# A spectral filter and a maxout layer on one core: the start-up of batch 0 and batch 1 replanned, filter split at two thirds, x in 8-token pieces

## The chip, the cores and the metric

The kernel runs on one NeuronCore of a Trainium2 chip. The metric is the device time of one execution in microseconds; the verdicts compare medians of runs of the two kernels on the same chip. The engines are named as in the profile: PE (TensorE matmuls), PEld (TensorE weight loads), DVE (VectorE), ACT (ScalarE), POOL (GpSimd) and SP (SyncE, which here only issues DMAs).

## What is computed

```python
def reference(x, filt_r, filt_i, moe_w1, moe_w2, moe_w_out):   # x: 8 x 3072 x 256 fp32
    X = np.fft.rfft(x, axis=1)                                 # 1537 frequencies, 256 channels
    Y = X * (filt_r + 1j * filt_i)[None]
    y = np.fft.irfft(Y, n=3072, axis=1).reshape(8 * 3072, 256)
    h1, h2 = y @ w1, y @ w2                                    # 256 -> 1024
    return np.maximum(h1, h2) @ w_out                          # 1024 -> 256
```

The kernel uses max(h1, h2) = h2 + relu(h1 - h2): Wd = w1 - w2, and M = w2 @ w_out goes straight from y to the output.

## The kernel before

**The transform.** 3072 = 96 x 32. A forward transform has two stages: f1 or s1 multiplies over the 96 rows (tables C1, CT), the result `at` goes to DRAM (`ad`) and is read back transposed as `bt`; s2 multiplies with the table U over the 32 columns and gives `px`. `product` multiplies px with the filter F (real and imaginary part) and gives `pq`. The inverse has s3 (tables VP and VQ), a copy `zt`, a way through DRAM (`zd`, read back as `zr` by z_read) and s4, which gives `y_`. A batch has six groups v of s2, product and s3; a *visit* n of a batch does s3 of group n-1, s2 and products of group n, and s1 for some chunks c ("quads") of the batch after it.

**Batch 0** does not go through DRAM: s1t, t1 (PE transposes into bt[0]), s2, products, s3t into zT and t2 (transposes into zr[0]), all written out in order at L538 to L614. Its x comes in eight POOL DMAs (`load_x`, L77, fp32 to bf16 on the way), the filter in eighteen (`load_f`, L95), in two halves h of six groups w each, one for the first and one for the second three v. The filter rows stand twice in F: `copy_f` doubles the first half on DVE, `dma_f` the second half by four SP DMAs. `fix_f` mends three rows on POOL. `stage_x` copies a px out of PSUM by ACT so that POOL can do a product; the groups in POOLED (L572) have their second product on POOL, the others on DVE. `spin(n)` is n matmuls whose result nobody reads, and s3t begins with one or two such matmuls (L497).

**Weights.** load_w reads w1 and w2 as fp32 (SP DMAs); w2 lies in two of the three buffers XF that later take x. prep_wd makes Wd on POOL in two halves, cast_w2 makes bf16 w2, prep_t and prep_m make M.

**The loop** (L665) has 64 blocks tt of 384 tokens, eight steps j each. A step does moe_h (two matmuls `ph` and a relu into gt, on DVE where `on_v` says so, else on ACT), then what `mid` plans for this step (the visits), then some matmuls `po` of moe_o of the block before, then what `todo` plans (f1, t2, reads, loads, folds). Steps are counted 0 to 63 within a batch of eight blocks. plan_f1 and plan_f2 put the work of the next batch on steps: f1 of batch 1 (16 chunks of two tokens, each reading half of an `xb` tile), f1_read (the bt read), the visits, z_read, s1_read, and for the batch after that load_xf (SP DMAs into XF) and fold (two POOL operations, sum and difference, into `xsd`).

**Order.** The schedule is by hand: every engine runs its instructions in the order of the code, and each DMA queue (SP's and POOL's) issues in that order too. A POOL or SP instruction that waits holds back all that stands behind it. SP issues F doubling, weights, ad writes, XF loads, bt and zr reads and zd writes; POOL issues x and filter loads, w_out and the output writes, and computes products, Wd, memsets and folds. POOL DMAs carry eight completion semaphores in turn, so the ninth waits for the first to land, and so on.

The lines that place batch 1's work in batch 0 are:

```python
    plan_f1(0, 1, (0, 1, 1, 2, 3, 3, 4, 5, 6, 7, 8, 8, 9, 9, 10, 10), 11)
    plan_f2(0, (22, 26, 30, 34, 38, 42, 46, 54), ((0, 1), (2,), (3,), (), (), (4,), (5,), (6, 7)),
            (8, 9, 10, 19, 21, 24, 27, 30), (13, 16, 19, 24, 27, 30, 33, 36))
```

Of the kernel before, what the change touches and what calls it, by code (L numbers as in the profile page):

```python
# [8 lines left out]
FP32 = mybir.dt.float32  # L9
BF16 = mybir.dt.bfloat16  # L10
# [16 lines left out]
def kernel(  # L27
# [34 lines left out]
    dram = ctx.enter_context(tc.tile_pool(name="dram", bufs=2, space=bass.MemoryType.DRAM))  # L62
    CT = const.tile([128, 2, 64], BF16)
    XF = [const.tile([128, 2, 2, D], FP32, name="XF%d" % k) for k in range(3)]
    xpool = ctx.enter_context(tc.tile_pool(name="xpool", bufs=8))
    bpool = ctx.enter_context(tc.tile_pool(name="bpool", bufs=2))
    pqpool = ctx.enter_context(tc.tile_pool(name="pqpool", bufs=6))
    ps = ctx.enter_context(tc.tile_pool(name="ps", bufs=6, space=bass.MemoryType.PSUM))
# [5 lines left out]

    xb = {}

    def load_x(b, c):  # L77
        t_ = xpool.tile([NP, 4, D], BF16, tag="xb", name="xb")
        src = x[b].rearrange("(p m) d -> p m d", m=NM)
        G.dma_start(out=t_, in_=src[:, 4 * c:4 * c + 4, :])  # L80
        xb[b, c] = t_

    def load_xf(b, c):
        src = x[b].rearrange("(h p m) d -> p h m d", h=2, m=NM)
        for g in range(2):
            nc.sync.dma_start(out=XF[(8 * b + c) % 3][64 * g:64 * g + 48], in_=src[:, :, 4 * c + 2 * g:4 * c + 2 * g + 2, :])

    def fold(b, c):
        t_ = xpool.tile([128, 2, 2, D], BF16, tag="xb", name="xsd")
        f = XF[(8 * b + c) % 3]  # L90
        G.tensor_tensor(t_[:, 0], f[:, 0], f[:, 1], OP.add)  # L91
        G.tensor_tensor(t_[:, 1], f[:, 0], f[:, 1], OP.subtract)  # L92
        xb[b, c] = t_

    def load_f(h):  # L95
        w0 = 6 * h
        for g in range(2):
            for ri, f in enumerate((filt_r, filt_i)):
                k0 = 24 * g + 2 * w0
                src = bass.AP(f.tensor, f.offset + k0 * D, [[96 * D, 16], [D, 12], [1, D]])  # L100
                G.dma_start(out=F[64 * g:64 * g + 16, ri, w0:w0 + 6].rearrange("p w s d -> p (w s) d"), in_=src)
                n0 = 1 if k0 == 0 else 0
                src = bass.AP(f.tensor, f.offset + (96 - k0 - n0) * D, [[96 * D, 16], [-D, 12 - n0], [1, D]])
                G.dma_start(out=F[64 * g + 16:64 * g + 32, ri, w0:w0 + 6].rearrange("p w s d -> p (w s) d")[:, n0:12],  # L104
                            in_=src)
                if n0:
                    src = bass.AP(f.tensor, f.offset + 48 * D, [[96 * D, 16], [1, D]])
                    G.dma_start(out=F[16:32, ri, 0, 0], in_=src)

    def copy_f(h, g, ri, engine):  # L110
        w0 = 6 * h
        o_, i_ = F[64 * g + 32:64 * g + 64, ri, w0:w0 + 6], F[64 * g:64 * g + 32, ri, w0:w0 + 6]
        if engine is S:
            S.activation(o_, i_, AF.Copy)
        else:
            engine.tensor_copy(o_, i_)

    def dma_f(h, g, ri):
        w0 = 6 * h
        nc.sync.dma_start(out=F[64 * g + 32:64 * g + 64, ri, w0:w0 + 6], in_=F[64 * g:64 * g + 32, ri, w0:w0 + 6])  # L120

    FN = init.tile([33, D], FP32)

# [19 lines left out]
    load_x(0, 0)  # L143
# [3 lines left out]
    load_x(0, 1)  # L147
# [3 lines left out]
    load_x(0, 2)  # L151
    G.iota(cid, pattern=[[1, 128]], base=0, channel_multiplier=0, allow_small_or_imprecise_dtypes=True)
    for c in range(3, 8):
        load_x(0, c)
    load_f(0)
    load_f(1)
    load_fn()
# [99 lines left out]
            S.activation((VQ if q else VP)[:, 6 * h:6 * h + 6, s], pv[s], AF.Copy)  # L257


    w1f = init.tile([128, 2, HID], FP32)  # L260
    w2f = [XF[h].rearrange("p c m d -> p c (m d)") for h in range(2)]

    def load_w(h):
        js = slice(512 * h, 512 * h + 512)
        nc.sync.dma_start(out=w1f[:, :, js], in_=moe_w1.rearrange("(c p) j -> p c j", p=128)[:, :, js])
        nc.sync.dma_start(out=w2f[h], in_=moe_w2.rearrange("(c p) j -> p c j", p=128)[:, :, js])

    def cast_w2(h, c):
        V.tensor_copy(w2b[:, c, 512 * h:512 * h + 512], w2f[h][:, c])

    def load_wo():
        G.dma_start(out=Wo, in_=moe_w_out.rearrange("(c p) j -> p c j", p=128))

    def prep_wd(h, engine):
        js = slice(512 * h, 512 * h + 512)
        engine.tensor_tensor(Wd[:, :, js], w1f[:, :, js], w2f[h], OP.subtract)

    def prep_t(jp):
        pt = ps.tile([128, 4, D], BF16, tag="ps", name="pt")
# [134 lines left out]
    gt = {}  # L414
    on_v = {(i, j) for i in range(8) for j in range(8)
            if (j in (1, 4, 6) if 2 < 8 * i + j < 11 else j in (1, 2, 4, 6, 7) if 8 * i + j < 22
                else j == 3 if 8 * i + j < 48 else j in (1, 3, 6))}

    def moe_h(tt, j):
        if j == 0:  # L420
# [73 lines left out]
    def s3t(v, pq):  # L494
        pool, tag = (ps, "ps") if v >= 4 else (pso, "po")
        pz = [pool.tile([128, 2, 2, 2, 2, NM], FP32, tag=tag, name="pt%d" % g) for g in range(2)]
        for _ in range(2 if v == 1 else 1):  # L497
            TE.matmul(pz[0].rearrange("p i s r c m -> p (i s r c m)"), W1[:, 0:128], W1, start=True, stop=True)
        for i in range(2):
            for s in range(2):  # L500
                for dc in range(2):
                    for q, tab in enumerate((VP, VQ)):
                        for g in range(2):
                            TE.matmul(pz[g][:, i, s, :, dc], pq[s][64 * g:64 * g + 64, q, i, 128 * dc:128 * dc + 128],  # L504
                                      tab[64 * g:64 * g + 64, 2 * v + i, s].rearrange("p (r m) -> p r m", r=2),
                                      start=(q == 0), stop=(q == 1))
# [34 lines left out]
    tables_u()  # L541
    for g in range(2):
        for ri in range(2):
            dma_f(1, g, ri)
    for h in range(2):
        load_w(h)
    spin(12)
# [9 lines left out]
    for n in range(6):  # L557
        t1(n, S if n % 2 else V)
    put_v(0, 0, table_v(0, 0))
    copy_f(0, 0, 0, V)  # L560
    copy_f(0, 0, 1, V)
    fix_f()
    copy_f(0, 1, 0, V)
    copy_f(0, 1, 1, V)
    xs = {}

    def stage_x(v):
# [1 line left out]
        S.activation(t_, pxs[v][1], AF.Copy)  # L569
        xs[v] = t_  # L570

    POOLED = (0, 2, 3)  # L572

    def products(v):
        pq = [product(V, v, 0, pxs[v][0])]
        pq.append(product(G, v, 1, xs[v]) if v in POOLED else product(V, v, 1, pxs[v][1]))
        return pq
# [16 lines left out]
    pxs[4] = s2(0, 4)  # L594
    pqs[3] = products(3)
    s3t(0, pqs[0])
    pxs[5] = s2(0, 5)
    load_x(1, 0)
    load_x(1, 1)
    pqs[4] = products(4)  # L600
    s3t(2, pqs[2])
    pqs[5] = products(5)
    for v in (3, 4, 5):
        s3t(v, pqs[v])
    spin(3)
# [11 lines left out]
    zpool = ctx.enter_context(tc.tile_pool(name="zpool", bufs=3))  # L617
    ypool = ctx.enter_context(tc.tile_pool(name="ypool", bufs=3))
    gpool = ctx.enter_context(tc.tile_pool(name="gpool", bufs=2))
    opool = ctx.enter_context(tc.tile_pool(name="opool", bufs=2))  # L620
    s4(0)
    spin(2)

# [88 lines left out]
```

## Time and profile before

| | us |
|---|---|
| median of 3 runs | 508.45 (506.44 to 508.6) |
| the profiled execution | 509.96 |
| its span in the profile | 508.2 |
| DVE, ACT, POOL busy | 331.0, 308.7, 259.6 |

The page also has the chain that ended last and the costliest groups:

```profile
PE 89%; DMA 4%; POOL 3%; DVE 1%; ACT 1%; issue 1%; SPq 0%; POOLq 0%; DVEq 0%
...
L452 PE MATMUL po<-Wo,gt 128*128 128x256 bf16 x1536 | 261.2, 273 | 0.0
L429 ACT ACTIVATE gt<-ph 128x384 bf16<-128x384 f32 x324 | 158.4, 495 | 144.4 <-PE ph L425 143.8
...
L365 DVE TENSOR_TENSOR pq<-px,F 128x1024 bf16<-128x1024 f32 x93 | 109.3, 1219 | 31.6 <-PE px L359 27.2
```

The first line shares out the chain by engine. A group's row has line, engine, operation, output and inputs, shape and count, then its busy time, the mean of one in ns, and the idle time of its engine just before it with what ended most of it.

### The profile page before, as it was taken

What the parts mean: (1) busy time and instruction counts of PE and PEld (TensorE: products, weight loads), DVE (VectorE), ACT (ScalarE), POOL (GpSimd) and SP (SyncE); (2) the same over time, 40 slices, a digit from 0 to 9 for tenths busy, and PEclk for the clock granted to TensorE, in tenths of its full rate; (3) what the DMA queues carried; (4) which work ended last, traced back from release to release, by engine and by line L of the source; (5) the groups of instructions that cost most, each with busy time, mean ns of one, the idle gap of its engine ahead of it and who ended that gap; (6) DMA issues with size and microseconds to landing.
All of it is one profiled execution on the core that took longest, in us unless ns stands there. A gap on an engine that the chain in (4) does not pass through costs nothing.

```text
span 508.2 us, 13046 instructions
## 1 busy us (share of the span) xinstructions
PE 492.7 (97%) x5302; PEld 364.0 (72%) x5305; DVE 331.0 (65%) x515; ACT 308.7 (61%) x628; POOL 259.6 (51%) x341
## 2 busy tenths in 40 slices
PE   7689989999999999999999999999999999999997
PEld 3456757777777777777777777777777777777775
DVE  7866668546875677557774677657774687555443
ACT  5756467766784576646774576646774465544442
POOL 6886378565645386539645466537742221222220
PEclk9858999999999999999999999999999999999999
DMA  7979697988799878895789778897769426511112
GB/s 123 172 219 177 206 300 220 253 253 193 219 251 238 185 245 219 243 261 167 214 229 239 191 233 183 260 232 201 218 177 227 117 105 166 165 65 63 63 63 83
DMA packets 75439, 97.06 MB, mean 191 GB/s; under 512 B 7314, under 2 KB 53651, under 8 KB 74707
## 3 DMA queue, kind: packets, MB, share of 16 engines
q1 hardware_dynamic: 61666, 66.60, 51.7%
q0 software_dynamic: 13712, 29.64, 20.4%
q8 instruction: 41, 0.67, 0.6%
q14 instruction: 20, 0.16, 0.1%
HBM read 53.48 MB, written 47.19 MB: 198 GB/s over the span
## 4 chain that ended last, share of the span: by engine, by line
PE 89%; DMA 4%; POOL 3%; DVE 1%; ACT 1%; issue 1%; SPq 0%; POOLq 0%; DVEq 0%
PE po L452 33%; PE ph L425 32%; PE po L450 8%; PE pz L376 5%; PE py L405 4%; PE pa L333 2%; PE px L359 2%; DMA xb<-in_x_dram 2%; DMA bt<-ad 1%; DVE pq L365 1%; DMA ad<-at 1%; POOL F L104 1%; PE pr L525 1%; POOL xb L80 1%; PE pt L504 1%
## 5 line engine op out<-in xcount | busy, mean ns | idle before, releaser
L452 PE MATMUL po<-Wo,gt 128*128 128x256 bf16 x1536 | 261.2, 273 | 0.0
L429 ACT ACTIVATE gt<-ph 128x384 bf16<-128x384 f32 x324 | 158.4, 495 | 144.4 <-PE ph L425 143.8
L438 POOL DMA_DIRECT2D out_dram<-ot x186 | 102.4, 555 | 183.3 <-DVE ot L464 176.6
L452 PEld LDWEIGHTS <-gt 128*128 128x128 bf16 x1536 | 146.5, 98 | 66.3 <-issue 10.7
L427 DVE TENSOR_SCALAR gt<-ph 128x384 bf16<-128x384 f32 x188 | 103.3, 553 | 64.2 <-PE ph L425 62.3
L365 DVE TENSOR_TENSOR pq<-px,F 128x1024 bf16<-128x1024 f32 x93 | 109.3, 1219 | 31.6 <-PE px L359 27.2
L425 PEld LDWEIGHTS <-Wd 128*128 128x128 bf16 x1024 | 96.7, 98 | 12.7 <-issue 1.1
L91 POOL TENSOR_TENSOR xsd<-XF 128x512 bf16<-128x512 f32 x48 | 61.2, 1276 | 43.5 <-DMA XF<-in_x_dram 13.4
L464 DVE COPY ot<-po 128x512 f32<-128x512 f32 x95 | 65.1, 685 | 24.3 <-PE po L452 19.2
L92 POOL TENSOR_TENSOR xsd<-XF 128x512 bf16<-128x512 f32 x48 | 61.0, 1271 | 0.0
L337 ACT ACTIVATE at<-pa 128x512 bf16<-128x512 f32 x96 | 51.7, 609 | 4.4 <-PE pa L333 4.1
L380 ACT ACTIVATE zt<-pz 128x512 bf16<-128x512 f32 x84 | 45.6, 595 | 11.4 <-PE pz L376 8.4
L405 PE MATMUL py<-G,zr 96*128 96x96 bf16 x512 | 32.7, 207 | 0.0
L405 PEld LDWEIGHTS <-zr 96*128 96x128 bf16 x512 | 29.2, 98 | 2.3 <-DVE zr L528 0.6
L359 PE MATMUL px<-bt,U 64*64 64x256 bf16 x384 | 20.4, 280 | 3.6 <-DMA bt<-ad 2.5
L376 PE MATMUL pz<-pq,VP 64*64 64x256 bf16 x336 | 21.9, 281 | 0.0
L376 PE MATMUL pz<-pq,VQ 64*64 64x256 bf16 x336 | 20.9, 269 | 0.0
L333 PE MATMUL pa<-xsd,CT 64*64 64x512 bf16 x192 | 19.3, 384 | 0.0
L376 PEld LDWEIGHTS <-VP 64*64 64x64 bf16 x336 | 9.7, 105 | 13.3 <-issue 13.3
L359 PEld LDWEIGHTS <-U 64*64 64x64 bf16 x384 | 10.4, 109 | 6.7 <-issue 3.7
L535 PE MATMUL pd<-W 128*128 128x512 bf16 x32 | 11.9, 488 | 1.8 <-DVE zero L137 1.5
L333 PEld LDWEIGHTS <-CT 64*64 64x64 bf16 x192 | 8.3, 105 | 2.4 <-ACT gt L429 1.2
(428 smaller groups left out, 609.7 us busy)
## 6 DMA issues: line engine op xcount, KB each, us to landing
out_dram<-ot POOLq DMA_DIRECT2D x186, 128.0 KB, 3.6
XF<-in_x_dram SPq DMA_DIRECT2D x96, 192.0 KB, 4.9
ad<-at SPq DMA_DIRECT2D x56, 192.0 KB, 3.8
bt<-ad SPq DMA_DIRECT2D x14, 768.0 KB, 11.5
zd<-zt SPq DMA_DIRECT2D x42, 256.0 KB, 2.9
zr<-zd SPq DMA_DIRECT2D x14, 768.0 KB, 7.8
xb<-in_x_dram POOLq DMA_DIRECT2D x16, 192.0 KB, 6.0
w1f<-in_moe_w_dram SPq DMA_DIRECT2D x2, 512.0 KB, 6.1
```

Source lines behind the costliest of these rows:

```text
L91: G.tensor_tensor(t_[:, 0], f[:, 0], f[:, 1], OP.add)
L92: G.tensor_tensor(t_[:, 1], f[:, 0], f[:, 1], OP.subtract)
L337: S.activation(at[:, m0:m0 + 2], pa[g], AF.Copy)
L365: E.tensor_tensor(pq, px.rearrange("p (o i) d -> p o i d", o=1).to_broadcast([128, 2, 2, D]), F[:, :, 2 * v:2 * v + 2, s], OP.mult)
L376: TE.matmul(pz[g][64 * s:64 * s + 64, i], tab[64 * g:64 * g + 64, 2 * v + i, s], pq[s][64 * g:64 * g + 64, q, i], start=(q == 0), stop=(q ...
L405: TE.matmul(py[:, m], zr[b][:, 4 * i + m, 128 * dc:128 * dc + 128], G1, start=True, stop=True)
L425: TE.matmul(ph, Wd[:, dc, 128 * j:128 * j + 128], y_[:, dc], start=(dc == 0), stop=(dc == 1))
L427: V.tensor_scalar(gt[tt][:, j], ph, 0.0, None, OP.max)
L429: S.activation(gt[tt][:, j], ph, AF.Relu)
L438: E.dma_start(out=dst, in_=ot[tt // 2][:, 3 * (tt % 2) + c])
L452: TE.matmul(p_, g_[:, n - 2, blk], Wo[:, n - 2], start=False, stop=(n == 9))
L464: V.tensor_copy(ot[tt // 2][:, e - 1:e + 1], po[0])
```

## The change

- `x_tile`: an xb tile holds eight tokens (two chunks) instead of four, in four buffers instead of eight. `load_x(b, c, n)` loads n chunks in one DMA; batch 0 comes as 1, 1, 2, 2, 2 chunks, batch 1 as four pairs. fold writes halves of such a tile.
- `WP`: the filter's first part has eight groups w (v = 0 to 3), the second four. `double_f` replaces copy_f and dma_f: the first part is doubled on DVE, the second by SP.
- The fp32 weights lie in `WS`, a tile of the zr pool, whose other buffer is zr[0]; XF is free of them.
- POOLED gets v = 4. s3t begins with two idle matmuls for v below 4; after s3t there is one spin fewer (two instead of three).
- In POOL's queue, all four pairs' and w_out's loads and the two prep_wd change order; table_ct (memsets of XF) goes from step 5 to step 2; opool is allocated earlier.
- Batch 0's plan: f1 on steps 0 to 8 instead of 0 to 10, the bt read at step 9 instead of 11, seven visits instead of eight, other steps for XF loads and folds; batch 1's loads and folds every 7 steps instead of 8.
- `on_v`: for blocks' steps 22 to 47 of batch 0, relus j = 1 and 5 on DVE instead of j = 3.

```diff
-    xpool = ctx.enter_context(tc.tile_pool(name="xpool", bufs=8))
+    xpool = ctx.enter_context(tc.tile_pool(name="xpool", bufs=4))
...
+    def x_tile(b, c):
+        if c % 2 == 0:
+            xb[b] = xpool.tile([128, 8, D], BF16, tag="xb", name="xb")
+        return xb[b][:, 4 * (c % 2):4 * (c % 2) + 4]
+
+    def load_x(b, c, n):
+        for k in range(c, c + n):
+            xb[b, k] = x_tile(b, k)[0:NP]
         src = x[b].rearrange("(p m) d -> p m d", m=NM)
-        G.dma_start(out=t_, in_=src[:, 4 * c:4 * c + 4, :])
-        xb[b, c] = t_
+        m0 = 4 * (c % 2)
+        G.dma_start(out=xb[b][0:NP, m0:m0 + 4 * n], in_=src[:, 4 * c:4 * c + 4 * n, :])
...
+    WP = ((0, 8), (8, 12))
+
     def load_f(h):
-        w0 = 6 * h
+        w0, w1 = WP[h]
+        n = 2 * (w1 - w0)
...
-    def copy_f(h, g, ri, engine):
...
-    def dma_f(h, g, ri):
...
+    def double_f(h, g, ri, engine):
+        w0, w1 = WP[h]
+        o_, i_ = F[64 * g + 32:64 * g + 64, ri, w0:w1], F[64 * g:64 * g + 32, ri, w0:w1]
+        if engine is V:
+            V.tensor_copy(o_, i_)
+        else:
+            nc.sync.dma_start(out=o_, in_=i_)
...
-    w1f = init.tile([128, 2, HID], FP32)
-    w2f = [XF[h].rearrange("p c m d -> p c (m d)") for h in range(2)]
+    WS = zrpool.tile([128, 4, HID], FP32, tag="zr", name="WS")
+    w1f, w2f = WS[:, 0:2], WS[:, 2:4]
...
-                else j == 3 if 8 * i + j < 48 else j in (1, 3, 6))}
+                else j in (1, 5) if 8 * i + j < 48 else j in (1, 3, 6))}
...
-        for _ in range(2 if v == 1 else 1):
+        for _ in range(2 if v < 4 else 1):
...
-    copy_f(0, 0, 0, V)
-    copy_f(0, 0, 1, V)
-    fix_f()
-    copy_f(0, 1, 0, V)
-    copy_f(0, 1, 1, V)
+    for g in range(2):
+        for ri in range(2):
+            double_f(0, g, ri, V)
+        if g == 0:
+            fix_f()
...
-    POOLED = (0, 2, 3)
+    POOLED = (0, 2, 3, 4)
...
+    stage_x(4)
     pxs[5] = s2(0, 5)
-    load_x(1, 0)
-    load_x(1, 1)
     pqs[4] = products(4)
+    for c in (0, 2):
+        load_x(1, c, 2)
     s3t(2, pqs[2])
     pqs[5] = products(5)
+    prep_wd(0, G)
     for v in (3, 4, 5):
         s3t(v, pqs[v])
-    spin(3)
-    prep_wd(0, G)
-    load_x(1, 2)
-    load_x(1, 3)
+    spin(2)
+    load_wo()
+    for c in (4, 6):
+        load_x(1, c, 2)
     prep_wd(1, G)
-    load_wo()
-    for c in range(4, 8):
-        load_x(1, c)
...
-    plan(0, 5, table_ct)
+    plan(0, 2, table_ct)
...
-    plan_f1(0, 1, (0, 1, 1, 2, 3, 3, 4, 5, 6, 7, 8, 8, 9, 9, 10, 10), 11)
-    plan_f2(0, (22, 26, 30, 34, 38, 42, 46, 54), ((0, 1), (2,), (3,), (), (), (4,), (5,), (6, 7)),
-            (8, 9, 10, 19, 21, 24, 27, 30), (13, 16, 19, 24, 27, 30, 33, 36))
+    plan_f1(0, 1, (0, 1, 1, 2, 2, 3, 3, 4, 4, 5, 6, 6, 7, 7, 8, 8), 9)
+    plan_f2(0, (22, 26, 30, 34, 38, 42, 46), ((0, 1), (2,), (3,), (4,), (5,), (6,), (7,)),
+            (6, 7, 11, 17, 19, 23, 26, 30), (13, 15, 18, 24, 27, 30, 33, 36))
     for b in range(1, B - 1):
         plan_f2(b, (7, 14, 18, 24, 31, 38, 42) if b > 1 else (14, 18, 24, 30, 34, 39, 42), ((0, 1), (2,), (3,), (4,), (5,), (6,), (7,)),
-                range(-32, 32, 8), range(-22, 42, 8))
+                range(-32, 32, 8) if b > 1 else range(-25, 31, 7), range(-22, 42, 8) if b > 1 else range(-15, 41, 7))
```

More of the change, by code (lines that the diff above doesn't have):

```diff
@@ L75 @@
     xb = {}
-    def load_x(b, c):
-        t_ = xpool.tile([NP, 4, D], BF16, tag="xb", name="xb")
+    def x_tile(b, c):
[5 more added lines that the diff above has]
+            xb[b, k] = x_tile(b, k)[0:NP]
         src = x[b].rearrange("(p m) d -> p m d", m=NM)
-        G.dma_start(out=t_, in_=src[:, 4 * c:4 * c + 4, :])
-        xb[b, c] = t_
+        m0 = 4 * (c % 2)
+        G.dma_start(out=xb[b][0:NP, m0:m0 + 4 * n], in_=src[:, 4 * c:4 * c + 4 * n, :])
     def load_xf(b, c):
@@ L85, in load_xf @@
         for g in range(2):
-            nc.sync.dma_start(out=XF[(8 * b + c) % 3][64 * g:64 * g + 48], in_=src[:, :, 4 * c + 2 * g:4 * c + 2 * g + 2, :])
+            nc.sync.dma_start(out=XF[(8 * b + c) % 3][64 * g:64 * g + 48],
+                              in_=src[:, :, 4 * c + 2 * g:4 * c + 2 * g + 2, :])
     def fold(b, c):
-        t_ = xpool.tile([128, 2, 2, D], BF16, tag="xb", name="xsd")
+        t_ = x_tile(b, c).rearrange("p (s m) d -> p s m d", s=2)
         f = XF[(8 * b + c) % 3]
@@ L99, in load_f @@
                 k0 = 24 * g + 2 * w0
-                src = bass.AP(f.tensor, f.offset + k0 * D, [[96 * D, 16], [D, 12], [1, D]])
-                G.dma_start(out=F[64 * g:64 * g + 16, ri, w0:w0 + 6].rearrange("p w s d -> p (w s) d"), in_=src)
+                src = bass.AP(f.tensor, f.offset + k0 * D, [[96 * D, 16], [D, n], [1, D]])
+                G.dma_start(out=F[64 * g:64 * g + 16, ri, w0:w1].rearrange("p w s d -> p (w s) d"), in_=src)
                 n0 = 1 if k0 == 0 else 0
-                src = bass.AP(f.tensor, f.offset + (96 - k0 - n0) * D, [[96 * D, 16], [-D, 12 - n0], [1, D]])
-                G.dma_start(out=F[64 * g + 16:64 * g + 32, ri, w0:w0 + 6].rearrange("p w s d -> p (w s) d")[:, n0:12],
+                src = bass.AP(f.tensor, f.offset + (96 - k0 - n0) * D, [[96 * D, 16], [-D, n - n0], [1, D]])
+                G.dma_start(out=F[64 * g + 16:64 * g + 32, ri, w0:w1].rearrange("p w s d -> p (w s) d")[:, n0:n],
                             in_=src)
@@ L108, in load_f @@
                     G.dma_start(out=F[16:32, ri, 0, 0], in_=src)
-    def copy_f(h, g, ri, engine):
[L111 to L114, printed above, removed]
-        else:
-            engine.tensor_copy(o_, i_)
-    def dma_f(h, g, ri):
-        w0 = 6 * h
-        nc.sync.dma_start(out=F[64 * g + 32:64 * g + 64, ri, w0:w0 + 6], in_=F[64 * g:64 * g + 32, ri, w0:w0 + 6])
+    def double_f(h, g, ri, engine):
[3 more added lines that the diff above has]
+            V.tensor_copy(o_, i_)
+        else:
+            nc.sync.dma_start(out=o_, in_=i_)
     FN = init.tile([33, D], FP32)
@@ L142 @@
     cid = init.tile([128, 128], FP32)
-    load_x(0, 0)
+    load_x(0, 0, 1)
     G.iota(pid, pattern=[[1, 1]], base=0, channel_multiplier=1, allow_small_or_imprecise_dtypes=True)
@@ L146 @@
            allow_small_or_imprecise_dtypes=True)
-    load_x(0, 1)
+    load_x(0, 1, 1)
     G.iota(kap, pattern=[[2, NW], [24, 2]], base=0, channel_multiplier=0,
@@ L150 @@
     G.iota(jb, pattern=[[1, 16]], base=0, channel_multiplier=0, allow_small_or_imprecise_dtypes=True)
-    load_x(0, 2)
+    load_x(0, 2, 2)
     G.iota(cid, pattern=[[1, 128]], base=0, channel_multiplier=0, allow_small_or_imprecise_dtypes=True)
-    for c in range(3, 8):
-        load_x(0, c)
+    for c in (4, 6):
+        load_x(0, c, 2)
     load_f(0)
@@ L265, in load_w @@
         nc.sync.dma_start(out=w1f[:, :, js], in_=moe_w1.rearrange("(c p) j -> p c j", p=128)[:, :, js])
-        nc.sync.dma_start(out=w2f[h], in_=moe_w2.rearrange("(c p) j -> p c j", p=128)[:, :, js])
+        nc.sync.dma_start(out=w2f[:, :, js], in_=moe_w2.rearrange("(c p) j -> p c j", p=128)[:, :, js])
     def cast_w2(h, c):
-        V.tensor_copy(w2b[:, c, 512 * h:512 * h + 512], w2f[h][:, c])
+        V.tensor_copy(w2b[:, c, 512 * h:512 * h + 512], w2f[:, c, 512 * h:512 * h + 512])
     def load_wo():
@@ L275, in prep_wd @@
         js = slice(512 * h, 512 * h + 512)
-        engine.tensor_tensor(Wd[:, :, js], w1f[:, :, js], w2f[h], OP.subtract)
+        engine.tensor_tensor(Wd[:, :, js], w1f[:, :, js], w2f[:, :, js], OP.subtract)
     def prep_t(jp):
@@ L543 @@
         for ri in range(2):
-            dma_f(1, g, ri)
+            double_f(1, g, ri, nc.sync)
     for h in range(2):
@@ L596 @@
     s3t(0, pqs[0])
+    stage_x(4)
     pxs[5] = s2(0, 5)
-    load_x(1, 0)
-    load_x(1, 1)
     pqs[4] = products(4)
+    for c in (0, 2):
+        load_x(1, c, 2)
     s3t(2, pqs[2])
     pqs[5] = products(5)
+    prep_wd(0, G)
     for v in (3, 4, 5):
         s3t(v, pqs[v])
-    spin(3)
-    prep_wd(0, G)
-    load_x(1, 2)
-    load_x(1, 3)
+    spin(2)
+    load_wo()
+    for c in (4, 6):
+        load_x(1, c, 2)
     prep_wd(1, G)
-    load_wo()
-    for c in range(4, 8):
-        load_x(1, c)
     t2(0, (V, S))
@@ L617 @@
     zpool = ctx.enter_context(tc.tile_pool(name="zpool", bufs=3))
+    opool = ctx.enter_context(tc.tile_pool(name="opool", bufs=2))
     ypool = ctx.enter_context(tc.tile_pool(name="ypool", bufs=3))
     gpool = ctx.enter_context(tc.tile_pool(name="gpool", bufs=2))
-    opool = ctx.enter_context(tc.tile_pool(name="opool", bufs=2))
     s4(0)
```

## The prediction

> **What bounds the kernel now.** I read the page first, then busy time by stage, then the timelines of the stages in which PE is not full, and the landings of single DMAs.
>
> ```profile
> span 508.2 us, 13046 instructions
> PE 492.7 (97%) x5302; PEld 364.0 (72%) x5305; DVE 331.0 (65%) x515; ACT 308.7 (61%) x628; POOL 259.6 (51%) x341
> ...
> 22.00:42.35 20.35, 16.46 (x316) 10.23 (x320) 12.90 (x15) 9.82 (x19) 17.70 (x17) 0.50 0.76 192
> 42.35:65.25 22.90, 22.36 (x195) 16.01 (x193) 16.47 (x31) 13.45 (x25) 10.37 (x15) 1.00 0.86 211
> 65.25:67.85 2.60, 0.12 (x2) 0.00 (x2) 0.00 (x0) 0.49 (x1) 2.58 (x5) 1.00 1.03 309
> 67.85:97.00 29.15, 29.15 (x378) 21.62 (x379) 21.84 (x26) 23.88 (x50) 21.37 (x23) 1.00 0.89 248
> 97.00:440.00 343.00, 343.00 (x3627) 256.33 (x3625) 230.59 (x337) 217.04 (x446) 175.55 (x222) 1.00 0.79 210
> ```
>
> The stage rows give us, then busy time of PE, PEld, DVE, ACT and POOL, the granted clock and the DMA share. From 67.85 us on PE is never idle up to its last matmul at 504.5, so no edit can win there; it can only lose. The change's whole effect is the moment from which PE is continuously full. Ahead of it stand two things: 20 us at half clock (0.50) and a hole of 2.6 us.
>
> ```profile
> 31.12 5.75 DVE L365 TENSOR_TENSOR pq<-px,F 128x1024 bf16<-128x1024 f32 x5 [4.24 <-DMA F<-F]
> ...
> 20.55 6.33 SPq L120 DMA_DIRECT2D F<-F  x4
> ...
> 40.91 2.26 POOL L80 DMA_DIRECT2D xb<-in_x_dram  x4
> ...
> 57.26 0.43 SPq L316 DMA_DIRECT2D ad<-at  x1
> ...
> 61.82 1.73 SPq L322 DMA_DIRECT2D bt<-ad  x2
> 63.59 4.92 SPq L86 DMA_DIRECT2D XF<-in_x_dram  x4
> ...
> 67.85 0.41 PE L359 MATMUL px<-bt,U 64*64 64x256 bf16 x8 [2.48 <-DMA bt<-ad]
> 72.88 0.39 PE L333 MATMUL pa<-xsd,CT 64*64 64x512 bf16 x4
> ```
>
> Columns: start, length, engine, line, operation, and in brackets the idle time before it and who ended it. DVE loses 4.24 us to the second filter half; PE's hole is the wait for bt, whose chain is the last ad write, its landing (4.5 us) and the read (6.0 us). The last row is the second visit's s1, the point against which I count.
>
> **The change, part by part.** All times are from the span's start.
>
> *x in 8-token pieces.* Last x landing now 14.11 (issue 6.18, 7.93 to land). In one piece with its neighbour it leaves s1t twice (0.34 apart) and two spins (0.43) to do: 0.8 late. POOL issues three DMAs of 0.53 fewer, which may land it earlier: between 0 and 0.8, I take +0.4.
>
> *Filter split.* DVE's four doublings cover 4096 instead of 3072 elements: 0.93 each becomes 1.24, +1.2 in all. They start at 18.43+0.4 and end at 23.8. The products follow at 1.15: the first pair ends at 26.1 (24.55 now). Five products, not four, precede the first that needs the second part, so DVE asks for it at 29.55. Now it lands at 26.38+4.6=31.0. POOL ends its issues some 1.5 earlier and the pieces are 128 KB, not 192: 28 to 31, I take 29.5, so DVE ends at 33.0 instead of 36.87.
>
> *Spins and PE.* That gain has no taker, because PE, cold, becomes the end. From the first s3t (26.85) follow: table 0.6, s2 0.65, then three s3t with two spins each (2 x 0.53 + 0.97), s2 0.64 and a wait of 0.65 for zT, and two s3t with one spin (1.50 each). That ends at 38.5 (37.7 now). The spin taken out later gives back 0.43. The first moe_h comes at 42.5, against 42.13.
>
> *Fourth Pool product, order of Pool.* ACT stages it only behind the copies of s3t(0) (ends 30.1): 1.08+0.6, so POOL runs it from 31.8 to 33.9 (2.13). Behind it in POOL's queue: two pairs of x, Wd half 0 (2.36, done 37.4, in time), Wo, two pairs, Wd half 1 (done 41.9; needed at step 4). The x landings: 3.3 fixed plus 0.97 per chunk (4.2 and 4.6 of the first two), so pairs at 39.1 and 41.0; Wo keeps the DMA engines 4.4 (from 41.9 to its landing at 46.27), hence 44.9; the third pair about 46.9. f1 chunk 8 is its reader.
>
> *f1 by step 8 instead of 10.* From c8 to c15 PE does 4.76 (48.54 to 53.3 now) plus what moved in between: s4 0.34, two prep_t 0.88, two ph 0.66, four f1 0.88, that is 7.5. If c8 waits for the pair, c15 ends at 54.4, against 55.86: 1.5 earlier. DVE and ACT have some 11 and 10 us of work in these nine steps against PE's 11, so they can take up to 1 of it.
>
> *bt read ahead.* From c15: copy and issue 1.4, write 3.75 to 4.5 (I take 3.75, the row of a write with two XF loads ahead of it, since the third now comes behind), so the read is issued at 59.6 and lands 5.2 to 6.0 later, 65.2. PE's own path from c15 to the first visit is 11.0, 65.4. The hole is gone: -2.45.
>
> *What is late next.* XF piece 2 (step 11) now queues on SP behind the bt read (step 9). The first XF behind bt took from 61.82 to 71.5, 9.7, its twin 0.5 more; less 0.8 for the loads no longer beside it, 9.4: 69.0. POOL's fold (two of 1.26) ends 71.5. s1 of the second visit, 5.03 behind the first, asks at 70.4. A new wait of 1.0, bounds 0 and 1.8 (without the 0.8). I take 0.5, below the middle, as the 9.7 is measured behind a read that began while four loads were still landing. So this s1 comes at 70.9, 16.5 after c15, where it is 72.88 now, 17.0 after c15. Behind it on POOL wait only out writes, whose ot has two buffers.
>
> *At nothing:* weights in the zr buffer and the earlier memset (POOL at 42 to 50, which nobody awaits before fold at 60); ACT to DVE, three more relus of 0.55 on DVE over 26 steps and four s1 earlier on ACT: DVE 21.8 and ACT 23.9 of 29.15 us in that stage leave room; if a burst closes it, 0.2 a visit, 1.4 at most. opool's place only moves addresses.
>
> **Sum.** -2.45+0.5 is -1.95. The profiled execution took 509.96, 1.76 around its span of 508.2; the median of the runs is 508.45, 1.5 below it. The span becomes 506.25 and the runs 506.5, that is -0.4%.
>
> **The rivals.**
>
> *The clock rises early* (0.23). PE's clock fell at about 21.9 and rose at 42.35, 20.4 us later. With the extra spins PE is without a break from 26.1 to 32.6. If it rises near 32.1, the last s3t ends at 35.5 instead of 38.5 and moe_h starts at 38.7. Where the x pairs are in time as well, c15 ends 12.4 later at 51.1 and the second visit's s1 comes at 51.1+16.5=67.6, 5.2 earlier: 503.2. For it: 39.0 to 42.35, full of spins, did raise the clock. Against: 28.8 to 32.1 was 85% busy and did not, and most of the new stretch is 64-row tiles; and a third pair landing at 46.9 takes it back to the forecast.
> The Trainium skill, TensorE: Matmul & The Clock Gate, Part 1: The HAM clock gate, says that one busy window of about 3.4 us frees the full clock and that the window runs free of the kernel; by it the break-free 6.5 us hold such a window. The trace agrees on the length (20.4 is six of them), not yet on what counts as busy.
>
> *The Pool queue runs late* (0.16, slower). The last filter issues, under DVE's doublings, took 1.05, 0.86 and 1.03 where earlier ones took 0.48 to 0.55, and two landed after 6.1 and 6.0 instead of 4. The doublings now last 5.0. If they hold the last four issues until 23.8, those end at 25.9, land at 31.9, and the doubling DMA at 36.6; the fourth product ends at 38.7 and everything behind it on POOL with it: third pair 51.7, c15 59.2, the second visit's s1 75.7, 2.9 later than now: 511.3. It decides from a product end of about 35.8. Against it: the issues were slowed, not stopped.
> The Trainium skill, SBUF — State Buffer, SBUF: two separate sides, says that a two-port VectorE copy locks GpSimd out so that it cannot write descriptors; by it this rival would be the rule. The slowed issues agree in kind, their 0.5 us in size does not.
>
> *It does nothing* (0.11). Clock cold, c15 at 42.5+12.4=54.9, the write 4.5 and the fold wait in full: 54.9+1.4+4.5+9.4+2.5=72.7, nearly the 72.88 of now: 508.3. The hole would only have moved.
>
> **Chances and range.** Forecast 0.50, of which 0.20 lie below 505.9. 0.5% is 2.5 us, about what a measurement of this kernel can tell from no change (the three runs lie within 2.2). Faster 0.20+0.23=0.43; same 0.30+0.11=0.41; slower 0.16. The range reaches from the early clock (503.0) to a Pool case of less than half its price (509.6); the forecast's own is 504.9 to 507.7.
>
> **What would show it.** Right: no 4.24 stall on DVE; the last s3t near 38 if the clock is still 0.50; a PE wait for xb near c8; bt landing within 0.5 of the first visit; a PE or POOL wait for XF near 70. Wrong: the clock at 1.00 by 33 and c8 unhindered (then faster), the last F issue after 23 (then slower), or any PE idle time after 75.

## The result: 6.6 us slower

The changed kernel takes 514.06 us (median of 6 runs, 512.56 to 515.34); the kernel before took 507.49 beside it (6 runs, 506.07 to 509.65). The ratio is 1.0125, 95% interval 1.0093 to 1.0157. The forecast was 506.5, range 503.0 to 509.6: the sign was wrong, and the time lies outside the range.

The profiled execution of the changed kernel took 514.36, its span 512.6. First the page, then the busy time by stage, in the same stages as before:

```profile
span 512.6 us, 13010 instructions
PE 492.4 (96%) x5302; PEld 363.9 (71%) x5307; DVE 337.9 (66%) x517; ACT 307.2 (60%) x626; POOL 262.1 (51%) x335
```

```profile
22.00:42.35 20.35, 14.85 (x332) 8.69 (x337) 15.33 (x15) 12.08 (x25) 19.30 (x16) 0.75 0.72 183
42.35:65.25 22.90, 19.43 (x145) 13.27 (x144) 16.66 (x25) 10.81 (x20) 9.56 (x10) 0.85 0.71 169
65.25:67.85 2.60, 2.60 (x26) 2.02 (x25) 2.19 (x4) 0.42 (x2) 2.60 (x3) 1.00 1.12 331
67.85:97.00 29.15, 28.33 (x360) 20.85 (x359) 23.26 (x30) 22.29 (x48) 22.32 (x24) 1.00 0.89 237
97.00:440.00 343.00, 341.92 (x3626) 255.61 (x3624) 229.91 (x336) 215.69 (x443) 177.83 (x224) 1.00 0.79 211
```

PE's busy time in the whole kernel is the same (492.4 against 492.7), so it is idle time that grew. The hole of 2.6 before bt is gone, as meant: PE is busy in all of 65.25 to 67.85. The first cold stretch is shorter: a clock of 0.75 over 20.35 us means half clock for 10.2 us, where it was all 20.35. But between 42.35 and 65.25 PE did 195 matmuls before and does 145 now, and the clock there is 0.85, so there is a second cold stretch of 6.9 us. After 67.85, where PE had no idle time before, 0.82 and 1.08 us are lost.

The timeline of DVE, and then that of POOL, of the changed kernel in the stage that lost (start, length, engine, line, operation):

```profile
40.74 3.09 DVE L276 CAST w2b<-WS 128x512 bf16<-128x512 f32 x1
43.75 0.54 DVE L434 TENSOR_SCALAR gt<-ph 128x384 bf16<-128x384 f32 x1
44.22 2.09 DVE L276 CAST w2b<-WS 128x512 bf16<-128x512 f32 x1
46.23 0.68 DVE L318 CAST at<-pa 96x512 bf16<-96x512 f32 x1
```

```profile
40.00 1.02 POOL L87 DMA_DIRECT2D xb<-in_x_dram  x2
41.03 4.99 POOL L283 TENSOR_TENSOR Wd<-WS 128x1024 bf16<-128x1024 f32 x1
45.97 3.56 POOL L181 MEMSET XF<- 128x1024 f32 x3
```

Before, the same cast took 0.42 us and Wd half 1 took 2.36, and the memsets waited for the casts (`<-DVE w2b`):

```profile
42.16 0.42 DVE L269 CAST w2b<-XF 128x512 bf16<-128x512 f32 x1
```

```profile
37.69 2.36 POOL L276 TENSOR_TENSOR Wd<-w1f,XF 128x1024 bf16<-128x1024 f32 x1
44.33 0.96 POOL L174 MEMSET XF<- 128x1024 f32 x1 [1.15 <-DVE w2b L269]
```

Now they run at the same time, and both are stretched: the first cast by 2.67, the second by 1.67, Wd by 2.63. The eviction at L318 and a relu at L434 stand behind the casts on DVE, and PE waits for them, as its waits of 38 to 67 us show (who waited for whom, us in total, times, longest):

```profile
PE pa L315 <- DVE at L318: 1.9, 1, 1.9
PE pa L315 <- DVE gt L434: 1.2, 1, 1.2
```

Before, this could not happen. Wd half 1 stood ahead of Wo in POOL's queue and was over at 40.05, two us ahead of the first cast; and w2 lay in XF, so the memsets of XF had to wait for the casts. The change moved the one behind the loads and took that guard from the other.

Two more delays can be seen in the same trace. The third pair of x, issued at 40.00, lands 8.9 us later, behind Wo (the DMA view of 39.90 to 40.45, which counts the issues that touch it; the last column is us to landing):

```profile
Wo<-in_moe_w_out_dram POOLq DMA_DIRECT2D x1, 512.0 KB, 8.0
xb<-in_x_dram POOLq DMA_DIRECT2D x1, 384.0 KB, 8.9
```

And after 67.85 PE waits for the fold of XF piece 2 (XF brings in the x of batch 2 in eight pieces, counted from 0) and for the second zr read:

```profile
PE py L412 <- DMA zr<-zd: 1.1, 1, 1.1
PE pa L340 <- POOL xb L99: 0.8, 1, 0.8
```

So the trace offers several causes. Which of them counts, and how much, the runs had to tell.

### The profile page after: what moved, and what is told of

Same layout as the page of the kernel before. It is cut to its first block, busy times and chain, and to the rows that moved or that the text cites. A ratio compares the mean times of both kernels' runs of the same rounds, so it can differ in the third digit from the quotient of the medians.

```text
span 512.6 us, 13010 instructions
## 1 busy us (share of the span) xinstructions
PE 492.4 (96%) x5302; PEld 363.9 (71%) x5307; DVE 337.9 (66%) x517; ACT 307.2 (60%) x626; POOL 262.1 (51%) x335
## 4 chain that ended last, share of the span: by engine, by line
PE 88%; DMA 5%; POOL 2%; DVE 1%; issue 1%; ACT 1%; POOLq 0%; SPq 0%
PE po L459 32%; PE ph L432 31%; PE po L457 8%; PE pz L383 4%; PE py L412 4%; PE pa L340 2%; PE px L366 2%; DMA xb<-in_x_dram 2%; DMA zr<-zd 2%; DMA F<-in_filt_r_dram 1%; DMA zd<-zt 1%; PE pt L511 1%; PE pa L315 1%; DVE w2b L276 1%; PE pr L532 1%
## 5 line engine op out<-in xcount | busy, mean ns | idle before, releaser
L436 ACT ACTIVATE gt<-ph 128x384 bf16<-128x384 f32 x321 | 156.7, 496 | 148.0 <-PE ph L432 147.4
L459 PEld LDWEIGHTS <-gt 128*128 128x128 bf16 x1536 | 146.6, 98 | 65.9 <-issue 10.2
L434 DVE TENSOR_SCALAR gt<-ph 128x384 bf16<-128x384 f32 x191 | 105.1, 554 | 64.3 <-PE ph L432 62.4
L98 POOL TENSOR_TENSOR xb<-XF 128x512 bf16<-128x512 f32 x48 | 61.2, 1274 | 50.7 <-DMA XF<-in_x_dram 29.6
L99 POOL TENSOR_TENSOR xb<-XF 128x512 bf16<-128x512 f32 x48 | 61.0, 1270 | 0.0
L340 PE MATMUL pa<-xb,CT 64*64 64x512 bf16 x192 | 20.1, 384 | 0.8 <-POOL xb L99 0.8
L542 PE MATMUL pd<-W 128*128 128x512 bf16 x31 | 10.8, 461 | 1.6 <-DVE zero L144 1.5
```

Of the source, the lines that this page charges most:

```text
L434: V.tensor_scalar(gt[tt][:, j], ph, 0.0, None, OP.max)
L436: S.activation(gt[tt][:, j], ph, AF.Relu)
L459: TE.matmul(p_, g_[:, n - 2, blk], Wo[:, n - 2], start=False, stop=(n == 9))
```

## The experiments

### Four first runs: the collision and the late pair, one at a time

a_cast_act takes the casts off DVE:

```diff
     def cast_w2(h, c):
-        V.tensor_copy(w2b[:, c, 512 * h:512 * h + 512], w2f[:, c, 512 * h:512 * h + 512])
+        S.activation(w2b[:, c, 512 * h:512 * h + 512], w2f[:, c, 512 * h:512 * h + 512], AF.Copy)
```

> The changed kernel with its four w2 casts (128x512, fp32 to bf16, all in SBUF) on ACT instead of DVE. Theory A (collision: the casts on DVE and POOL's Wd half 1 and XF memsets, now at the same time, lock each other out, DVE is late with the evictions, PE idles and its clock falls): Wd half 1 back from 4.99 to about 2.4 us, the three memsets from 3.56 to about 2.8, no PE idle time above 0.5 us between 41 and 48 us, no second stretch at half clock; 514.06 falls by 5 to 6.5, to 507.6 to 509. Theory B (the third and fourth pair of x land late, at 48.9 and 50.7): nothing changes, 513 to 514.5. Theory C (nine steps instead of eleven are too much for DVE, collision or not): DVE is rid of 4 x 0.42 = 1.7 us, so 512 to 513.

Measured 513.88 (4 runs), ratio to before 1.0118 (1.0067 to 1.0170): no gain, as theory B had it, although the lengths that theory A gave for Wd and the memsets came true. POOL's timeline has both operations at their old lengths; PE's has a new wait in the same place, and the second stretch at half clock is still there (a clock of 0.65 over 46 to 54 us and 0.92 over 54 to 62, again 6.9 us):

```profile
40.92 2.36 POOL L283 TENSOR_TENSOR Wd<-WS 128x1024 bf16<-128x1024 f32 x1
43.21 2.75 POOL L181 MEMSET XF<- 128x1024 f32 x3
```

```profile
46.57 0.38 PE L315 MATMUL pa<-xb,C 96*96 96x512 bf16 x1 [0.24 <-ACT at L320]
49.16 0.66 PE L315 MATMUL pa<-xb,C 96*96 96x512 bf16 x1 [2.21 <-DMA xb<-in_x_dram]
```

Chunk 8 now asks at 46.95 and gets its x at 49.1, the time at which the collision had let PE go on anyway. So neither theory alone holds: the two delays lie side by side.

a_wd_first puts Wd half 1 directly behind Wd half 0:

```diff
     prep_wd(0, G)
+    prep_wd(1, G)
...
-    prep_wd(1, G)
```

> The changed kernel with Wd half 1 directly behind Wd half 0 in POOL's queue, so that Wo and the last two pairs of x are issued 2.4 us later. Theory A: Wd half 1 takes 2.4 us from 39.1 and is over before the first cast; the memsets alone meet the casts, so about half of the loss of 6 comes back: 510 to 512. Theory B (late x): the last pairs land at about 51.3 and 53, PE waits 2 us longer at chunk 8: 515 to 516.5. Theory C: unchanged, 513.5 to 514.5.

Measured 514.12 (4 runs), 1.0143 (1.0095 to 1.0191), at theory C's figure, but not for its reason. The first cast was not over early, it was held still longer:

```profile
39.76 6.11 DVE L276 CAST w2b<-WS 128x512 bf16<-128x512 f32 x1
```

```profile
40.75 0.93 POOL L279 DMA_DIRECT2D Wo<-in_moe_w_out_dram  x1
41.68 1.02 POOL L87 DMA_DIRECT2D xb<-in_x_dram  x2
42.69 2.76 POOL L181 MEMSET XF<- 128x1024 f32 x3
```

It came while POOL still ran Wd, and ended 0.42 after the last memset (42.69 + 2.76 = 45.45), as if it had not begun before POOL's whole row of instructions was done. The late x shows as well: PE waits 3.1 us behind this cast and then 2.3 us for x.

b_wd_last makes one move in the kernel before:

```diff
-    prep_wd(1, G)
     load_wo()
     for c in range(4, 8):
         load_x(1, c)
+    prep_wd(1, G)
```

> The kernel before with one thing moved: Wd half 1 goes behind Wo and the last four x loads in POOL's queue, so it would run from about 40.9 us, as in the changed kernel, and meet the first casts (42.16, 43.79); the memsets still wait for the casts. Theory A: the first cast takes 1.5 to 3 us instead of 0.42, Wd half 1 more than 3 us, and the kernel is 1.5 to 4 us slower than before: 509 to 511.5. Theories B and C: the x loads come 2.4 us earlier and the plan is the old one, so the same or faster: 506 to 507.5.

Measured 512.96 (4 runs), 1.0111 (1.0057 to 1.0166). Slower, 1.5 beyond the range of theory A, and for another reason: the casts took 0.41 to 0.42.

```profile
42.92 0.56 DVE L411 TENSOR_SCALAR y__975<-py 128x384 bf16<-128x384 f32 x1 [3.78 <-POOL Wd L276]
43.39 0.41 DVE L269 CAST w2b<-XF 128x512 bf16<-128x512 f32 x1
```

DVE waits 3.78 us for POOL's Wd before it may write y: the pool of y lies where w1 lay, and Wd half 1 is the last to read w1. This run says nothing of the collision. It does say what the weights' move in the change is good for: with it Wd half 1 can stand late without holding y.

b_ws makes only that move, in the kernel before: the lines of `WS`, load_w, cast_w2 and prep_wd as in the change, all else old.

> The kernel before with only the fp32 weights moved to the idle zr buffer. XF is then free of them and the memsets no longer wait for the casts: they run behind the last x issue, from 43.2 us, beside casts two to four. Theory A: these three casts take about 0.7 to 2 us each instead of 0.42 and the memsets over 3 us in all; slower than before by 0.5 to 2.5: 508 to 510. Theories B and C: no difference, 507 to 507.8.

Measured 512.11 (6 runs), 1.0092 (1.0056 to 1.0128): 4.6 us slower than before, 2 more than theory A said. The memsets no longer wait for the casts, and the second cast is held until they are over, and PE behind it:

```profile
41.06 4.57 DVE L269 CAST w2b<-WS 128x512 bf16<-128x512 f32 x1
```

```profile
40.43 2.03 POOL L80 DMA_DIRECT2D xb<-in_x_dram  x4
42.43 2.78 POOL L174 MEMSET XF<- 128x1024 f32 x3
```

```profile
PE pa L308 <- DVE at L311: 3.8, 1, 3.8
```

Again it ends 0.42 after the last memset (45.21). This is the single part of the change that the forecast put at nothing, alone in the kernel before.

### Both taken out, and the replan alone

a_cast_wo has the casts on ACT and moves Wo between the last two pairs; a_wo_mid has only the second:

```diff
-    load_wo()
-    for c in (4, 6):
-        load_x(1, c, 2)
+    load_x(1, 4, 2)
+    load_wo()
+    load_x(1, 6, 2)
```

> The changed kernel with both suspects taken out: the w2 casts on ACT, and Wo issued between the last two pairs of x instead of ahead of them. Theory D (two delays lie side by side in the first nine steps, the collision of the casts with POOL, and the third x pair, which lands at 49 because Wo keeps the DMA engines 5 us ahead of it; either one alone leaves PE idle some 2 to 3 us and drops its clock for 6.8 us): the third pair lands at 43.5 to 45, the wait of 2.2 at chunk 8 is gone, the clock does not fall a second time or not before 50; 513.88 falls by 4 to 6, to 508 to 510. Theory C (the nine steps are too crowded whatever feeds them): PE waits for evictions instead, 512 to 514.

> The changed kernel with Wo between the last two pairs of x only; the casts stay on DVE. Theory D: the third pair lands at 43.5 to 45, but the collision alone still holds DVE and PE until about 47 and drops the clock: no gain, 513 to 514.5. A theory that the late pair is the whole cause: 508 to 510.

a_cast_wo: 510.31 (7 runs), 1.0060 (1.0035 to 1.0085), 0.3 beyond theory D's range. a_wo_mid: 513.38 (4 runs), 1.0120 (1.0084 to 1.0156), no gain, as theory D had it. The pair is then in time, but the collision still holds PE. Only both together help. In a_cast_wo PE has no wait over 0.5 from the first moe_h to 70 us; then it stops for XF piece 2. Its waits of 60 to 122 us, and SP's and POOL's timelines:

```profile
PE pa L340 <- POOL xb L98: 1.7, 1, 1.7
PE pa L340 <- POOL xb L99: 0.8, 1, 0.8
```

```profile
60.48 1.16 SPq L329 DMA_DIRECT2D bt<-ad  x2
61.69 6.30 SPq L92 DMA_DIRECT2D XF<-in_x_dram  x6
```

```profile
72.26 1.25 POOL L98 TENSOR_TENSOR xb<-XF 128x512 bf16<-128x512 f32 x1 [4.68 <-DMA XF<-in_x_dram]
```

Piece 2 stands behind the bt read on SP, and POOL sits idle for 4.68 us until it is there, at 72.26. The bt read is issued 2.2 us earlier than in the changed kernel (60.48 against 62.71), but the fold of piece 2 begins only 1.5 earlier (72.26 against 73.75): a third wall.

a_fill puts idle matmuls into PE's two waits in the changed kernel:

```diff
+        for _ in range({4: 5, 5: 9}.get(c, 0)):
+            pd = pso.tile([128, 512], FP32, tag="po", name="pd")
+            TE.matmul(pd, W1[:, 0:128], W1, start=True, stop=True)
```

> The changed kernel with 14 idle matmuls (128x512, about 0.21 us each at full clock, their results unused) put into the two waits of PE between 42 and 47 us, five ahead of chunk 4 and nine ahead of chunk 5. They take away no wait, only the idle time. If the second stretch at half clock (6.8 us, worth 3.4) comes from these waits: clock 1.00 from the first rise to the end, 510 to 511.5. If it does not hang on them: still a second stretch at 0.50, 514 to 515.

Measured 515.31 (4 runs), 1.0146 (1.0106 to 1.0186). The profiled execution is the fastest of the four (512.63; the others 514.56 to 516.41). Its clock is 1.00 in every stage from 38 to 440 us, so there the second cold stretch was gone; what the clock did in the other three is not known by stage. Nor were the waits the same: in this trace Wd kept its 2.36 and the first cast was held for 3.90, to the end of the memsets. XF and zr still make PE wait (0.7 and 1.4), and the nine matmuls, 1.9 us, can outlast the wait that they fill. What the cold stretch by itself is worth stays open.

b_replan makes only the other large part of the change, in the kernel before: plan_f1, plan_f2 and on_v of batch 0 (and batch 1's steps for XF) as in the change.

> The kernel before with only batch 0 planned as in the changed kernel (f1 by step 8, bt read at step 9, 7 visits, XF loads and folds, relus); POOL's order, filter and weights as before, so casts and POOL do not meet. Theory D: chunk 8 is asked for at step 4, about 46.5 to 47.5, and its x lands at 47.6, so a wait of 0 to 1; the hole before bt (2.5) is gone, the waits for XF (0.8) and zr (1.1) are there: 505.5 to 508. If the replan itself is the loss, because nine steps are too few for DVE and ACT: 510 to 513.

Measured 511.16 (6 runs), 1.0062 (1.0040 to 1.0084): in the range for "the replan itself is the loss", but not because DVE and ACT are too busy. PE waits for x:

```profile
43.43 0.38 PE L308 MATMUL pa<-xb,C 96*96 96x512 bf16 x1
46.54 0.66 PE L308 MATMUL pa<-xb,C 96*96 96x512 bf16 x1 [2.73 <-DMA xb<-in_x_dram]
```

Chunk 8, moved from step 6 to step 4, asks at 43.8; its x is issued at 40.00 behind Wo and takes 6.5. The loads were not moved with it.

### The third wall, and the parts put back one by one

a_cast_wo_xf is a_cast_wo with XF piece 2 ahead of the bt read; a_all also moves the last two visits, (38, 42, 46) to (38, 41, 44):

```diff
-            (6, 7, 11, 17, 19, 23, 26, 30), (13, 15, 18, 24, 27, 30, 33, 36))
+            (6, 7, 8, 17, 19, 23, 26, 30), (13, 15, 18, 24, 27, 30, 33, 36))
```

> The changed kernel with the casts on ACT, Wo between the last two x pairs, and XF piece 2 at step 8, ahead of the bt read, instead of step 11 behind it. Theory E (three walls in a row: collision, x pair, and XF piece 2, which lands at 72 to 74 in every run so far because SP holds its two DMAs some 3 to 8 us behind the bt read): piece 2 lands before 65, the waits for its fold (1.7 + 0.8) are gone, bt lands at most 1.5 later and nobody waits for it; 510.31 falls by 2 to 2.5, to 507.5 to 508.5; the wait for zr (1.1 to 1.4, seen where there was no XF wait before it) may come back. If XF is only the next name of some other delay: 509.5 to 511.

> The same, and the last two visits of batch 0 one and two steps earlier (41, 44), so that the second zr read is issued two steps earlier. Theory E: no PE wait above 0.5 us after 62 us is left; 0.5 to 1.4 below the kernel without it, 506.5 to 508. If the zr wait was a by-product of late XF pieces, no difference.

a_cast_wo_xf: 506.15 (10 runs), 0.9971 (0.9937 to 1.0004), 4.2 less than a_cast_wo, more than expected. The wait that went was 2.5, so the rest is not shown to come from it: the two kernels ran beside different runs of the kernel before (507.14 and 507.67, which makes the gain 3.6), and the mean clock of a_cast_wo's runs was 0.983 to 0.987, that of a_cast_wo_xf's 0.986 to 0.992. a_all: 506.85 (10 runs), 1.0000 (0.9972 to 1.0028): no difference, so the zr wait had only been a consequence. In a_cast_wo_xf the longest waits of PE from 42 to 122 us are these:

```profile
PE ph L432 <- ACT at L320: 0.4, 1, 0.4
PE pa L315 <- ACT at L320: 0.2, 1, 0.2
```

PE is fed throughout; that is what the change had been forecast to reach, and 506.15 is near the 506.5 of the forecast; but its interval includes 1, so a gain over the kernel before is not shown.

b_best repairs the replan in the kernel before: x 4 and 5 ahead of Wo, XF piece 2 at step 8, the last visits as in a_all.

> The kernel before with the replanned batch 0 and its three walls removed: x 4 and 5 ahead of Wo, XF piece 2 at step 8, the last two visits at 41 and 44. The casts do not meet POOL here, because Wd half 1 comes first and XF's memsets wait for the casts. Theory E: no wait for x at chunk 8 (2.7 before), none for XF (0.8), no hole before bt; against the 511.16 of the replan alone 3.5 to 6.5 less: 504.5 to 507.5, that is the same as the kernel before or up to 3 faster. If nine steps are too few for DVE and ACT: above 509.

Measured 507.59 (10 runs), 1.0004 (0.9972 to 1.0037). The three waits are gone, but Wo now comes late for M, and PE waits 2.39 for it. That is a gap in the expectation: what is moved ahead of Wo makes Wo late.

b_start has only the startup part in the kernel before (x pieces, filter split, spins, fourth product).

> The kernel before with only the startup part: x in 8-token pieces, filter split at two thirds, the extra idle matmuls, the fourth POOL product; weights and plan of batch 0 as before, Wd half 1 ahead of Wo. The forecast had this part at +0.4 to the first moe_h (PE becomes the end of the startup instead of the filter). Theory E: the losses are elsewhere, so 506.5 to 508.5; if the startup carries part of the loss, above 509; if it is the gain that the rest hides, below 506.

Measured 509.85 (10 runs), 1.0067 (1.0038 to 1.0097). That is above 509, but in its trace PE waits 1.2 for y, which stands behind Wd half 1 as in b_wd_last, 1.4 for x and 2.3 for bt. The startup part cannot be judged without the weights' move; the run leaves its own worth open.

The last runs put the walls back into the repaired kernel, and one more takes the x pieces apart.

> The repaired kernel (casts on ACT, Wo between the last x pairs, XF piece 2 at step 8; 506.15) with Wo put back ahead of both pairs. Theory E: the third pair lands at about 49 again and PE waits about 2 us for it at chunk 8; with the clock it loses 2 to 5: 508 to 511. If the late pair has no price of its own: 506 to 507.

> The repaired kernel with the casts back on DVE. Theory E: the collision returns (a cast of 3 us and one of 2, Wd half 1 of 5, PE idle about 3 us between 42 and 47, clock down for 3 to 7 us): it loses 3 to 6: 509 to 512. If the collision only ever hid behind the late x pair: 506 to 507.5.

> The changed kernel with only XF piece 2 moved to step 8. Theory E: the two earlier walls stand, and behind them the wait for piece 2 was 0.8 to 1.1, so it gains 0.5 to 2: 512 to 513.5. If XF were the main cause: 508 to 510.

a_cast_xf, only the x pair late: 511.62 (10 runs), 1.0072 (1.0038 to 1.0107), a loss of 5.5 on 506.15, 0.6 above the range. a_wo_xf, only the collision: 511.83 (10 runs), 1.0093 (1.0060 to 1.0125), a loss of 5.7, within the range. a_xf, both: 512.50 (4 runs), 1.0102 (1.0033 to 1.0171), a loss of 6.4, within the range. The kernel before ran at 506.82 beside these three and at 507.14 beside the repaired kernel, so by the ratios the losses are rather larger. Either delay alone costs nearly as much as both: they fill the same time. The wait in a_cast_xf's trace is longer than the 2 expected:

```profile
44.47 0.38 PE L315 MATMUL pa<-xb,C 96*96 96x512 bf16 x1 [0.25 <-ACT at L320]
48.83 0.66 PE L315 MATMUL pa<-xb,C 96*96 96x512 bf16 x1 [3.99 <-DMA xb<-in_x_dram]
```

and its clock falls again behind it:

```profile
38.00:46.00 8.00, 6.09 (x45) 3.45 (x46) 5.49 (x11) 5.96 (x12) 7.89 (x10) 1.00 1.13 176
46.00:54.00 8.00, 5.17 (x33) 3.69 (x34) 1.76 (x3) 2.90 (x5) 0.26 (x1) 0.57 0.64 173
```

> The repaired kernel with x of batch 0 loaded in 4-token pieces again (8 issues instead of 5), all else as repaired. In the profile of the kernel before t1 began at 15.09, with 8-token pieces at 16.0 to 16.25, and PE ends the startup; so if that 0.9 is the cost of the larger pieces it comes back: 505 to 505.8. If the filter, whose issues now come 1.6 us later on POOL, ends the startup instead: 506 to 508.

> The repaired kernel with x of batch 0 in 4-token pieces once more, in more rounds, since the interval just reached 1.0001. If the 1 us it showed against the kernel before is real: ratio 0.996 to 0.999 with an interval below 1. If not: an interval around 1.

a_x4: 505.76 (10 runs), 0.9969 (0.9936 to 1.0001), within the lower range expected. In more runs: 506.04 (12 runs), 0.9986 (0.9963 to 1.0010). So no version was found that is measurably faster than the kernel before; the repaired ones equal it.

The ladder in one table (each ratio is to the runs of the kernel before beside it):

| kernel | median us | ratio to before |
|---|---|---|
| changed kernel | 514.06 | 1.0125 |
| casts on ACT | 513.88 | 1.0118 |
| Wo between the pairs | 513.38 | 1.0120 |
| XF piece 2 ahead of bt | 512.50 | 1.0102 |
| casts and Wo | 510.31 | 1.0060 |
| casts and XF | 511.62 | 1.0072 |
| Wo and XF | 511.83 | 1.0093 |
| all three | 506.15 | 0.9971 |

## Why the prediction was wrong

**The step that failed is "At nothing".** It put "weights in the zr buffer and the earlier memset" at nothing because nobody awaits POOL at 42 to 50. True, nobody waits for POOL's results there; but DVE waits for POOL itself. The step asked who awaits the moved instructions and not whom they run beside. "Fourth Pool product" asked the same of Wd half 1, "needed at step 4", and it ran from 41.03 to 46.02 beside the casts. By b_ws the move of the weights alone costs 4.6 us; in the otherwise repaired kernel the collision costs 5.7 (a_wo_xf). The Trainium skill, SBUF — State Buffer, SBUF: two separate sides, says that the ports shared by VectorE and GpSimd are an exclusive lock, and that the one that comes second blocks. The forecast weighed this page for the filter copies, where the last issue came at 21.81, before the 23 it named, and did not carry it to the casts. There a cast that was held for 4.57 (b_ws) or 6.11 us (a_wd_first) instead of 0.42 agrees with it in kind; in the changed kernel neither side was blocked outright, and both were stretched (3.09 and 4.99).

**"Fourth Pool product": the term of the third x pair was mis-sized, and this alone costs as much.** It was put at 46.9 and landed at 48.9, while the first moe_h came at 40.64 instead of 42.5. Most of the 2.0 stems from POOL's queue: its first product began at 26.50 (24.54 before), behind the last filter issue and `fix_f`, so ACT's copies of s3t(0) ended at 33.0 instead of 30.1; the fourth product ended at 35.70 instead of 33.9, Wo was issued at 39.07 instead of 37.4 and landed at 47.1 instead of 44.9 (a figure that the 41.0 and 4.4 beside it do not add up to). The wait for c8 became 2.2 (a_cast_act) to 4.0 (a_cast_xf), and the sum let PE run on at full clock behind it, where the clock of a_cast_xf fell to 0.57 over 46 to 54 us. Since the collision held PE as long, the late pair did not show in the changed kernel's own waits; alone it costs 5.5 (a_cast_xf).

**"What is late next" named the right wait with too small a price.** It reckoned 9.4 from the bt issue to the landing of piece 2, where its fold can begin; the fold began after 11.0 in the changed kernel (62.71 to 73.75, a trace that does not show the landing) and after 11.8 in a_cast_wo (60.48 to 72.26, right behind the landing). The wait was 0.8 in the changed kernel, and 2.5 in a_cast_wo, where all else is on time; in a_cast_wo_xf, with the piece moved, the wait is gone. The forecast took 0.5 of a range of 0 to 1.8. For the wait for zr, 1.1 at 112.75, it had no term; idle time of PE behind 75 was one of its own signs of being wrong.

**"f1 by step 8"** therefore failed as a sum: c15 was to end at 54.4, with the last ad write issued 1.4 behind it, and that write is issued at 59.91, later than the 57.26 of before. DVE's 11 us of work in these steps had been added up from undisturbed rows.

**Right:** that the effect lies in when PE is full and not in its work (492.4 against 492.7 us busy); that the filter stall of 4.24 goes (five products in a row, 24.22 to 29.97, without a wait); that the hole before bt goes. The price of the x pieces, 0.4, was 0.9 at t1 (16.00 against 15.09) and could not be told in time.

**The rivals.** The clock rose early, as the first rival had it, at about 33; but the spins are not shown to be the reason. b_ws has the old spins, and over 22 to 38 us its clock is 0.79, half clock for 6.7 us; a_cast_act has the new ones, and its clock there is 0.58, half clock for 13.4 us. How long the cold stretch lasts differs from run to run: the mean clock in the other runs of the kernel before was 0.980 to 0.997, and 0.978 in the profiled one. So the sum was made against an execution with an unusually long cold stretch, and an early clock is no gain against the median. The slower rival, a late POOL queue through the filter issues, came in part: the last three filter issues took 0.89, 1.13 and 1.28, and the fourth product ended at 35.70, 1.8 behind the forecast and 0.1 short of the 35.8 from which it decides. That was luck, not a margin. DVE and POOL holding each other up, on which this rival rested, cost its time twenty us later.

## What to carry to other kernels

When an edit frees a buffer or reorders a queue, list what could not overlap before and now can: a dependency that looks like a cost may be what keeps two engines out of each other's way. When work is moved to an earlier step, move its loads with it, and look for the next transfer in line each time a wait is removed. Two delays of one length in one place look like one, and taking away either alone shows nothing.

## What the runs showed of the hardware

A cast on DVE from SBUF to SBUF (128x512, fp32 to bf16, 0.42 us alone) that meets POOL at work can be held not for one instruction but for a row of them: 6.11 us across the rest of Wd, three DMA issues and three memsets. Reads from PSUM on DVE beside POOL's work were not stretched (the relu at 43.75 took 0.54). In the changed kernel the cast began first (40.74 against 41.03), and both were stretched: 3.09 instead of 0.42 and 4.99 instead of 2.36. The same order and the same Wd (5.00 to 5.01) stand in a_wo_mid, a_wo_xf and a_xf; in a_wd_first and a_fill, where Wd was running first, it kept its 2.3 to 2.4 and the cast was held to the end of the memsets. DMA issues of POOL alone did not hold a cast: before, the one at 42.16 took 0.42 while POOL issued x (40.91 to 43.17). Why the cast of b_ws, which began during such issues, was held through them and the memsets behind them stays open.

Behind waits of PE between 42 and 51 us the clock fell to half a second time in many runs: for 6.9 us in the changed kernel (waits of 1.2 and 1.9), a_cast_act (2.2), b_replan (2.7) and a_cast_xf (3.99; 0.57 over 46 to 54 us), and for 3.4 us in a_wo_mid (0.9 and 1.9) and b_best (2.4), both with 0.79 over 46 to 54 us. Behind a wait of 2.5 in the kernel before (65.25 to 67.85) and one of 2.3 in b_start it stayed at 1.00, so the length of a wait alone does not decide. The Trainium skill, TensorE: Matmul & The Clock Gate, Part 1: The HAM clock gate, speaks of a free-running window of about 3.4 us; 10.2, 6.9 and 3.4 are three, two and one of them, and a stretch of 6.5 us without a break need not hold a whole one, as the prediction took it to.
